# Sparse attention and a Mish MLP on one core: two products joined into one of 129 columns, in another order of work

## The chip, the cores and the metric

One core of a Trainium2 chip runs the whole program. The metric is the time of one execution on the device in microseconds; lower is better. The engines are PE (TensorE; its weight loads are PEld), DVE (VectorE), ACT (ScalarE), POOL (GpSimd) and SP (SyncE, which here only issues DMAs).

## What is computed

Block-sparse attention over 4 batches, 8 heads, 768 positions, 64 dimensions per head, and then an MLP without biases over the 3072 resulting rows of 512:

```python
block, n_blocks = 32, 24
scores = (q @ k.T) / 8
# a block of 32 queries sees: its neighbours (distance <= 1), the first and the last block,
# and 3 sampled blocks; the first and the last block of queries see everything
scores = where(mask, scores, -1e9)
attn = exp(scores - max); attn = attn / (sum(attn) + 1e-9)
x = (attn @ v) laid out as [3072, 512]
h = x @ w_in                       # [3072, 2048]
out = (h * tanh(softplus(h))) @ w_out
```

All inputs are float32. The kernel multiplies in float16 in three products: every operand is split into a high and a low half, and high by high, low by high and high by low are added up in float32.

## The kernel before

**Attention** is cut into 52 jobs, 13 for each batch. Two of the 13 are dense (the first and the last block of queries, 768 keys each, in three steps of 256, `nt = 3`; of these jobs 0, 10, 13, 23, 26, 36, 39 and 49); the other 44 are pairs of neighbouring query blocks (`nt = 2`, one step for each block, 256 gathered keys each). A job is a chain over the engines. PE computes the scores S of all 8 heads (L674); DVE takes the maximum (L737); ACT the exponential into pt (L756); PE transposes (L680); ACT writes the high half of the transposed probabilities, ph (L779), DVE the low half, pl (L783; up to job 5 PE subtracts in PSUM and ACT copies, L787 and L792). Then PE does the O block (L818): with 32 columns of ph or pl as weights on one of four column strips, it multiplies gathered values. A row of values holds, for each head, 64 high halves, a one, 64 low halves and a zero, so a product of 65 columns gives the output's high part and the sum of the probabilities in one, and another of 64 columns the part of the low halves. All O blocks write the same PSUM bank, `obank`; a job has up to four regions in it, numbered by the query block w and the half g of a pair of heads. DVE then takes the reciprocal of the sums and scales (`xs_fn`: r at L837, L838, xs at L840), PE transposes back (tx, L680 again), and ACT and DVE split the result into the halves xh and xl (L864, L867), which the MLP reads.

**The MLP** runs over 12 tiles of 256 rows, two passes on PE: h (L1068, eight steps of 2 x 12 products) and y (L1162). The last four tiles use a folded form of the second pass (L1281: seven products over sums of blocks instead of eight, some of them in obank). Between the passes ACT, DVE and POOL compute Mish (L1079 to L1148) and the halves g and, for the folded form, the sums' halves sg (L1144 and L1148).

**Weights** come in by DMA (`load_w`, L893; w_in as wr, w_out as wor), and are decoded and split by DVE and ACT before the first product of L1068 (L901 to L907, L962, L968; gsc at L1035).

**Order.** Every step is a task with a number. `Plan.add` registers it with its engine, and for some a second possible engine; `ORDER`, a table of numbers at the end of the file, says in which order the tasks are written out and, with a letter b, that the second engine does it. Each engine executes its instructions strictly in that order, waits included; DMA issues stand in the streams of SP or ACT. In a word such as `172+33` the number after the plus makes `fill` (L1502 on) issue that many products of 240 columns into columns of obank that nobody reads, ahead of the task; they stand only where no O block is open. A constant `SPLIT = 10` says from which job on an O block is one task instead of one for each step.

The O block and the scaling, as they were:

```python
o, w = tl[ko], 0 if dense else j                 # obank as [P, 2, 2, 66]
for n, (p, v0, v1) in enumerate(((hi, 0, D + 1), (hi, D + 1, 2 * D + 1), (lo, 0, D + 1))):
    for c in range(NPR):
        nc.tensor.matmul(o[cs, w, g, 0:v1 - v0], p[:, k, g, cs], vt[:, k, 2 * c + g, v0:v1], ...)
...
nc.vector.tensor_tensor(out=xs, in0=o[:, 0:nsu, :, 0:D], in1=r.unsqueeze(3).to_broadcast([P, nsu, 2, D]), op=ALU.mult)
```

Of the kernel before, what the change touches and what calls it, by code (L numbers as in the profile page):

```python
# [14 lines left out]
ALU = mybir.AluOpType  # L15
# [6 lines left out]
PSC = 4096.0  # L22
# [197 lines left out]
def attn_mish_kernel(ctx: ExitStack, tc: tile.TileContext, qT, kT, v, sampled, blocks, w_in, w_out, out):  # L220
# [119 lines left out]
    NO, NZ = 4 * (D + 2), 240  # L340
# [315 lines left out]

# [41 lines left out]
    def attend(job):  # L698
# [108 lines left out]
        def o_fn(j):  # L807
            if j == 0:
                tl[ko] = obank[:, 0:NO].rearrange("p (w g d) -> p w g d", w=2, g=2)
            o, w = tl[ko], 0 if dense else j  # L810
            vt = vgs[sus[w]["ng"] % NVG] if not dense else tl["vt", b, j] if sus[0]["qb"] else tl["v", b, j]
            hi, lo = tl["ph", i, j], tl["pl", i, j]
            for g in range(2):
                for k in range(2):
                    for n, (p, v0, v1) in enumerate(((hi, 0, D + 1), (hi, D + 1, 2 * D + 1), (lo, 0, D + 1))):
                        for c in range(NPR):
                            cs = slice(c * BS, (c + 1) * BS)
                            nc.tensor.matmul(  # L818
                                o[cs, w, g, 0:v1 - v0], p[:, k, g, cs], vt[:, k, 2 * c + g, v0:v1],
                                start=j == 0 and g == 0 and k == 0 and n == 0,  # L820
                                stop=j == nt - 1 and g == 1 and k == 1 and n == 2)
# [12 lines left out]
        def xs_fn():  # L834
            o = tl[ko]
            r = new(sb, "r", ("r", i), [P, nsu, 2])
            nc.vector.tensor_scalar(out=r, in0=o[:, 0:nsu, :, D], scalar1=PSC * 1e-9, scalar2=None, op0=ALU.add)  # L837
            nc.vector.reciprocal(out=r, in_=r)  # L838
            xs = new(at_, "xs", ("xs", i), [P, nsu, 2, D])
            nc.vector.tensor_tensor(  # L840
                out=xs, in0=o[:, 0:nsu, :, 0:D], in1=r.unsqueeze(3).to_broadcast([P, nsu, 2, D]), op=ALU.mult)
        add("DVE", 0.8, xs_fn, r=[ko], w=[("r", i), ("xs", i)], new=[("r", ("r", i)), ("xs", ("xs", i))], key=-1.5)

        def tx_fn():
            tx = new(ps["t"], "t", ("tx", i), [P, nsu, P])
            for w in range(nsu):
                transpose(tx[:, w], tl["xs", i][:, w].rearrange("p g d -> p (g d)"), w == 0, w == nsu - 1)
# [721 lines left out]
    456 484 1629 268b 506 439 1638 457 440 485 257 486 235 1640 243 248 487 1630 488 253 441 164 458 442 489 459 482  # L1569
    510 1631b 254 1639 1641 511 529 1632 460 527 81 512 289 491 490 1651 500 492 285 78 1633 269 493 507 461 1652 513  # L1570
    249 1634 1642 290 514 515 258 494 286 462 495 1653 509 255 531 1643 270 1654 259 1635b 250 463 516 528 1655 1636
    496 501 517 518 532 1665 519 591 1656 272b 520 533 276b 497 1657 1644 291 292 89 521 251 498 522 1645 530 534 499
    293 523 1666 535 271 536 1668 1658 537 280b 273 1646 548 1659 538 524 1669 525 1667 526 1647 287 294 539 593 1660
    1679 1648 540 1680 1661 541 1649b 1662 551 1670 542 1650 552 1663b 543 1684 550 1671 549 544 1664 1685 553 1681
    554 295 1697 274 555 281 277 1698 275 1686 1672 464 1687 556 278 559 1702 279 560 557 561 1673b 296 282 297 298
    1688 299 1699 562 283 1674 300 1703 1689 558 563 1675 564 301 302 303 545 1717 1676 546 465 547 565 1704 304 1677
    466 1678 305 588 1718 306 467 566 590 307 1722 309b 1690 308 1723 310 1719 1691 313b 468 1735 311 469 314 1724 502
    1736 317 503 318 504 1740 312 321 1692 315 1682 1705 322 316 1683 325 505 470 1741 319 326 570 320 329 1695 323
    330 1696 324 333 589 327 334 592 567 1700 328 337 331 338 595 1725 332 1701 596 614 335 594 568 336 597 1713 598
    611 569 615 634 1714 599 612 90 1706 571 600 473b 1715 603 617 1716 604 613 601 1720 1707 618 572 602 619 1721 573  # L1580
    476b 605 620 606 1726 471 1733 616 1727b 477b 574 472 1734 621 575 607 1708 622 625 623 1693 1738 626 624 1694
    1728 627 1739 474 608 1729 576 478 628 1737 1751 629 609 610 475 630 1752 631 1709 632 1755 580 1753b 1710 1742
    1758 584 1730 1711b 585 640 636 635 1756 581 641 1712 1731b 1760 1743 582 1759 642 1757 665 659 577 586 1761 1754
# [127 lines left out]
```

## Time and profile before

| | |
|---|---|
| median of 3 runs | 754.28 us (751.87 to 755.23) |
| profiled execution | 754.41 us, its span 752.6 us |
| busy: PE, PEld, DVE, ACT, POOL | 708.4, 543.4, 548.1, 579.3, 281.7 us |
| mean granted clock of PE | 0.984 |
| chain that ended last, by engine | PE 82%, DVE 7%, DMA 4%, issue 3% |
| O blocks, S blocks on that chain | 6%, 5% |

The span is one execution's first to last instruction; 1.8 us of the execution lie around it. Granted clock 1.00 is 2.4 GHz, 0.50 is 1.2 GHz. A busy PE counts a product from its start to its modelled end, and since products overlap, what one costs in a row of them is read from the distance of their starts, as the chain of waits gives it. "issue" is time in which an engine waited for nothing that the profile shows.

### The profile page before, as it was taken

To read this page: it belongs to the slowest core of one execution; us is meant where nothing else is said; L and a number is where in the kernel's file an instruction comes from. 1 tells how busy PE (TensorE), PEld (TensorE's weight loads), DVE (VectorE), ACT (ScalarE), POOL (GpSimd) and SP (SyncE) were. 2 spreads that over 40 slices of the span, in tenths; PEclk is the share of its full clock that TensorE was granted. 3 is DMA by queue.
4 is the path that set the end of the run, shared out by engine and by line. 5 is a ranking of instruction groups with operands and counts; after the bars stand their busy time and mean duration, and the time that the engine had idled before them with its cause. 6 is when DMAs were issued, how large, how long until landed. Compare 5 with 4: busy or idle time off the path is not lost.

```text
span 752.6 us, 31176 instructions
## 1 busy us (share of the span) xinstructions
PE 708.4 (94%) x13023; PEld 543.4 (72%) x13023; DVE 548.1 (73%) x1015; ACT 579.3 (77%) x927; POOL 281.7 (37%) x380
## 2 busy tenths in 40 slices
PE   5567798999999999999999999999999999999997
PEld 4455577875776776777676776677677778888887
DVE  5869878897667856977767757877886855577665
ACT  2648677999796788887877789886887786787783
POOL 2004234517754551244543454564374301200140
PEclk9889899999999999999999999999999999999999
DMA  8788766533235273247337353344532447000001
GB/s 302 249 250 245 227 212 179 198 121 88 108 112 167 83 251 103 93 132 217 91 104 229 102 213 108 82 142 144 159 88 72 145 131 245 16 1 15 16 29 43
DMA packets 60050, 103.75 MB, mean 138 GB/s; under 512 B 8579, under 2 KB 20868, under 8 KB 59908
## 3 DMA queue, kind: packets, MB, share of 16 engines
q1 hardware_dynamic: 54576, 88.90, 37.9%
q10 hardware_dynamic: 5332, 12.85, 5.2%
q8 instruction: 102, 1.67, 0.9%
q14 instruction: 40, 0.33, 0.1%
HBM read 84.58 MB, written 17.14 MB: 135 GB/s over the span
## 4 chain that ended last, share of the span: by engine, by line
PE 82%; DVE 7%; DMA 4%; issue 3%; SPq 2%; ACT 1%; POOLq 0%; ACTq 0%; POOL 0%; DVEq 0%
PE h_None L1068 31%; PE y L1162 21%; PE yr L1281 8%; PE obank L818 6%; PE t L680 6%; PE s L674 5%; DMA vg<-vd 2%; PE obank L1281 1%; PE tx L680 1%; DMA raw_k<-in_k_dram 1%; DVE hs_None L1107 1%; DMA raw_q<-in_q_dram 1%; SPq L580 1%; DVE v L504 1%; ACT pt L756 1%
## 5 line engine op out<-in xcount | busy, mean ns | idle before, releaser
L1068 PEld LDWEIGHTS <-wi 128*128 128x128 f16 x2304 | 223.8, 98 | 38.6 <-issue 5.4
L1068 PE MATMUL h_None<-xh,wi 128*128 128x256 f16 x1152 | 208.1, 274 | 3.2 <-issue 3.2
L611 POOL COPY kg<-kt 128x256 f16 x246 | 112.5, 491 | 163.2 <-PE s L674 146.3
L1162 PE MATMUL y<-wo,g 128*128 128x512 f16 x672 | 159.1, 379 | 0.0
L1068 PE MATMUL h_None<-xl,wi 128*128 128x256 f16 x576 | 157.6, 274 | 0.0
L1120 POOL TENSOR_TENSOR g<-hs_None,g 128x1024 f16<-128x1024 f32 x36 | 81.0, 2251 | 131.3 <-ACT g L1114 85.7
L1162 PEld LDWEIGHTS <-g 128*128 128x128 f16 x768 | 74.1, 98 | 70.8 <-issue 1.1
L756 ACT ACTIVATE pt<-s,nb,ns 128x256 f32<-128x256 f32 (+1 forms) x208 | 107.4, 584 | 1.3 <-DVE wi L907 0.9
L779 ACT ACTIVATE ph<-t 128x512 f16<-128x512 f32 x112 | 66.1, 600 | 47.1 <-PE t L680 39.2
L783 DVE SCALAR_TENSOR_TENSOR pl<-t,ph 128x512 f16<-128x512 f32 x99 | 67.0, 684 | 35.0 <-ACT ph L779 34.8
L680 PE MATMUL t<-ident,pt 128*128 128x128 f32 x448 | 68.9, 280 | 9.3 <-ACT pl L792 4.4
L1107 DVE SCALAR_TENSOR_TENSOR hs_None<-us_None,hs_None 128x1024 f32<-128x1024 f32 x48 | 62.7, 1307 | 18.9 <-ACT us_None L1106 17.6
L1079 ACT ACTIVATE hs_None<-h_None,gsc 128x512 f32<-128x512 f32 x96 | 66.0, 687 | 13.6 <-PE h_None L1068 13.6
L737 DVE TENSOR_REDUCE mx<-s 128x4 f32<-128x1024 f32 x44 | 53.7, 1220 | 27.8 <-PE s L674 27.8
L1068 PE MATMUL h_None<-xr,wi 128*128 128x256 f16 x576 | 67.8, 273 | 0.0
L680 PEld LDWEIGHTS t<-ident,pt 128*128 128x128 f32 x448 | 52.3, 143 | 21.3 <-ACT pl L792 5.7
L818 PEld LDWEIGHTS <-ph 128*32 128x32 f16 x3584 | 47.8, 94 | 14.7 <-issue 12.9
L1098 ACT ACTIVATE us_None<-hs_None,hsc 128x1024 f32<-128x1024 f32 x48 | 55.4, 1154 | 1.6 <-DVE sg L1148 1.1
L818 PE MATMUL obank<-vg,ph 128*32 128x65 f16 (+1 forms) x3200 | 49.1, 196 | 2.6 <-issue 2.3
L1105 ACT ACTIVATE us_None<-us_None 128x1024 f32<-128x1024 f32 x48 | 50.9, 1059 | 0.3
L1106 ACT ACTIVATE us_None<-us_None 128x1024 f32<-128x1024 f32 x48 | 50.7, 1060 | 0.4
L818 PEld LDWEIGHTS <-pl 128*32 128x32 f16 x1792 | 46.5, 96 | 5.7 <-issue 3.8
(258 smaller groups left out, 1202.9 us busy)
## 6 DMA issues: line engine op xcount, KB each, us to landing
vg<-vd SPq DMA_DIRECT2D x320, 65.0 KB, 2.6
vg<-vd SPq DMA_DIRECT2D x80, 195.0 KB, 3.2
wr<-in_moe_w_in_dram ACTq DMA_DIRECT2D x7, 1024.0 KB, 6.3
vd<-v SPq DMA_DIRECT2D x12, 520.0 KB, 4.2
vg<-vd SPq DMA_DIRECT2D x12, 520.0 KB, 5.3
raw_k<-in_k_dram SPq DMA_DIRECT2D x12, 512.0 KB, 5.8
raw_q<-in_q_dram SPq DMA_DIRECT2D x12, 512.0 KB, 4.4
raw_v<-in_v_dram SPq DMA_DIRECT2D x12, 512.0 KB, 4.9
```

The source lines that it names most:

```text
L611: nc.gpsimd.tensor_copy(out=dst, in_=tl["kt", b][:, :, ds(j, BS)])
L680: nc.tensor.matmul(out, src, ident, start=start, stop=stop, is_transpose=True)
L756: ex = lambda o, x, g, w: nc.scalar.activation(out=o, in_=x, func=AF.Exp, bias=nb[:, g, w:w + 1], scale=tl["ns", b, sus[w]["qb"] // TB][:, ...
L779: nc.scalar.activation(out=new(at_, "ph", ("ph", i, j), [P, 2, 2, P], F16), in_=tl["t", i, j], func=AF.Copy, scale=PSC)
L783: nc.vector.scalar_tensor_tensor(out=new(at_, "pl", ("pl", i, j), [P, 2, 2, P], F16), in0=tl["t", i, j], scalar=PSC, in1=tl["ph", i, j], o ...
L818: nc.tensor.matmul(o[cs, w, g, 0:v1 - v0], p[:, k, g, cs], vt[:, k, 2 * c + g, v0:v1], start=j == 0 and g == 0 and k == 0 and n == 0, stop ...
L1068: nc.tensor.matmul(h[:, f2, 0:n].rearrange("p (s q) -> p s q", q=BS), wi[:, fp, w, cc, fs], x[:, s0:s0 + sn, cc], start=f2 == 0 and k == 0 ...
L1079: nc.scalar.activation(out=tl[kq][:, 2 * (fp % 2):2 * (fp % 2) + 2, 0:n], in_=tl[kh][:, :, 0:n], func=AF.Copy, scale=gsc[:, fp:fp + 1])
L1107: add("DVE", 1.32 * c, lambda: nc.vector.scalar_tensor_tensor(out=hs(), in0=us(), scalar=-0.5, in1=hs(), op0=ALU.add, op1=ALU.mult), r=[ku ...
L1120: add("POOL", 2.3 * c, lambda: nc.gpsimd.tensor_tensor(out=g(1), in0=hs(), in1=g(0), op=ALU.subtract), r=[kq, ("gh",) + kp], w=[kp], use=[kg],
L1162: nc.tensor.matmul(tl[ky], tl["g", b, t, k][:, g, f, q], wo_at(fc)[:, w], start=fc == 0 and n == 0, stop=fc == NFC - 1 and n == 2)
L1281: nc.tensor.matmul(R(i), lhs, rhs, start=head and j == n == 0, stop=k == NFC // 4 - 1 and j == 1 and n == 2, skip_group_check=True)
```

## The change

From job 10 on the products of ph with the high and with the low halves of the values are one product of 129 columns, in three of the four regions: 65 columns as before and right beside them the 64 of the low halves. The regions are then 130 columns apart in place of 66; the fourth has no room in the bank's 512 columns for the second part, and keeps the three products. The low part is no longer added up on PE; DVE scales it by r, too, and adds it (`add_lo`, two more instructions a job). xs becomes a flat tile of 7 x 64, of which the last three parts hold the scaled low part.

```diff
-    NO, NZ = 4 * (D + 2), 240
+    NO, NZ, OP = 4 * (D + 2), 240, (D + 2, 2 * (D + 1))
...
+    def add_lo(xs, t, o, r):
+        nc.vector.tensor_tensor(out=t, in0=o, in1=r, op=ALU.mult)
+        nc.vector.tensor_tensor(out=xs, in0=xs, in1=t, op=ALU.add)
...
-                tl[ko] = obank[:, 0:NO].rearrange("p (w g d) -> p w g d", w=2, g=2)
-            o, w = tl[ko], 0 if dense else j
+                tl[ko] = obank
+            w, apart = 0 if dense else j, i >= SPLIT
...
-            for g in range(2):
-                for k in range(2):
-                    for n, (p, v0, v1) in enumerate(((hi, 0, D + 1), (hi, D + 1, 2 * D + 1), (lo, 0, D + 1))):
-                        for c in range(NPR):
...
+            for g, k in ((g, k) for g in range(2) for k in range(2)):
+                at, whole = (OP[apart] * (2 * w + g), apart and w + g < 2)
+                prods = ((hi, 0, 2 * D + 1), (lo, 0, D + 1)) if whole else ((hi, 0, D + 1), (hi, D + 1, 2 * D + 1), (lo, 0, D + 1))
+                for n, (p, v0, v1) in enumerate(prods):
+                    for cs, c in ((slice(c * BS, (c + 1) * BS), c) for c in range(NPR)):
+                        nc.tensor.matmul(
+                            obank[cs, at:at + v1 - v0], p[:, k, g, cs], vt[:, k, 2 * c + g, v0:v1],
...
-            xs = new(at_, "xs", ("xs", i), [P, nsu, 2, D])
-            nc.vector.tensor_tensor(
-                out=xs, in0=o[:, 0:nsu, :, 0:D], in1=r.unsqueeze(3).to_broadcast([P, nsu, 2, D]), op=ALU.mult)
+            nc.vector.tensor_tensor(out=xs[:, 0:m], **dict(zip(("in0", "in1"), part(0, m))), op=ALU.mult)
+            add_lo(xs[:, 0:min(m, 3)], xs[:, 4:4 + min(m, 3)], *part(D + 1, min(m, 3))) if i >= SPLIT else None
...
 ORDER = """
-    7 1 0 8 2 9 3 4 53 74 5 6 67 10 85 11 12 14 51 13 15 18 76 16 17 28 92 19 20 22 117b 29 21 61 24 23 75 30+5 93 77
+    7 1 0 2 3 5 8 4 9 10 60 11 12 6 13 64 14 18 88 15 117b 16 20 69 17 19 93b 28 22 56 29 76 21 24 84 30 77 23 63 99b
```

The table ORDER is another one throughout, from another seed, and has no word with a plus. Counted over the whole program it moves, besides the above: all 17 weight loads of ACT's stream to SP's; 7 squares of L1103 from POOL to ACT (L1104), 4 copies of g from ACT to DVE (L1116), and a few more single steps from one engine to its second.

The O block of job 11, a pair, in PE's stream before (each row stands four times, once for each column strip, and the three groups again for the other seven combinations of query block, g and k):

```order
L818 LDWEIGHTS ph_11_0_5499
L818 MATMUL obank_109<-vg0_115,ph_11_0_5499 32x65
...
L818 MATMUL obank_109<-vg0_115,ph_11_0_5499 32x64
L818 LDWEIGHTS pl_11_0_5514
L818 MATMUL obank_109<-vg0_115,pl_11_0_5514 32x65
```

The same place in the change (the second half are the last rows of the block, the fourth region):

```order
L818 LDWEIGHTS ph_11_0_5327
L818 MATMUL obank_109<-vg0_115,ph_11_0_5327 32x129
L818 LDWEIGHTS pl_11_0_5366
L818 MATMUL obank_109<-vg0_115,pl_11_0_5366 32x65
...
L818 LDWEIGHTS ph_11_1_5350
L818 MATMUL obank_109<-vg1_116,ph_11_1_5350 32x65
L818 MATMUL obank_109<-vg1_116,ph_11_1_5350 32x64
L818 MATMUL obank_109<-vg1_116,pl_11_1_5352 32x65
```

Of 96 pairs of a weight load and a product 72 are left. In the whole program PE has 3584 products of 65 columns and 1792 of 64 before, 2408, 616 and 1176 of 129 after.

PE's stream around the transposes of job 0's output (tx_0), before, with two of the places at which fills (neg into obank) stand:

```order
L373 MATMUL gram_wi_1_1074<-wi_71 128x128
L396 MATMUL tp_w_0_1093<-wq_0_923,ones_69 128x2
L1506 LDWEIGHTS neg_73
L1506 MATMUL obank_109<-neg_73 128x240
L680 MATMUL tx_0_1109<-ident_64,xs_0_1091 128x128
...
L870 MATMUL tx_0_1109<-xh_0_0_1135,neg_73 128x128
```

and in the change:

```order
L373 MATMUL gram_wi_2_1091<-wi_71 128x128
L680 MATMUL t_1_1_1115<-ident_64,pt_1_866 128x128 x4
L680 MATMUL tx_0_1123<-ident_64,xs_0_1076 128x128
L674 LDWEIGHTS q_0_0_305
L674 MATMUL s_2_1128<-kt_0_230,q_0_0_305 32x96
```

The fills are gone here and everywhere (113 of them), and S of job 2 follows at once.

ACT's stream while jobs 0 and 1 run, before, with two of the weight loads (wr):

```order
L608 ACTIVATE kg1_114<-kt_0_259 128x8x32
L893 DMA wr_4_1065<-in_moe_w_in_dram 128x4x512
L962 ACTIVATE wi_71<-wi_71,ws_0_1095 128x1024
...
L756 ACTIVATE pt_1_1138<-s_1_746,nb_1_1133,ns_0_0_277 128x256 x2
L893 DMA wr_7_1187<-in_moe_w_in_dram 128x4x512
L779 ACTIVATE ph_1_0_1288<-t_1_0_1179 128x512
```

and SP's in the change, where these loads stand now:

```order
L893 DMA wr_6_810<-in_moe_w_in_dram 128x4x512
L571 DMA vg1_116<-vd0_60 32x1040 x2
L571 DMA vg0_115<-vd0_60 32x1040 x2
L893 DMA wr_4_917<-in_moe_w_in_dram 128x4x512
L580 TENSOR_LOAD offv_87
...
L571 DMA vg2_117<-vd0_60 32x1040 x2
```

ACT's ph no longer stands behind a load; the gathers of values (vg) and the register loads (L580) do.

## Rows read from the trace of the kernel before

**Rows 1.** The page's part 1: busy time and share of each engine.

```profile
PE 708.4 (94%) x13023; PEld 543.4 (72%) x13023; DVE 548.1 (73%) x1015; ACT 579.3 (77%) x927; POOL 281.7 (37%) x380
```

**Rows 2.** Stretches: busy us and count of PE, PEld, DVE, ACT, POOL; granted clock; DMA.

```profile
60.00:85.00 25.00, 19.44 (x671) 14.34 (x656) 23.77 (x52) 20.28 (x44) 10.21 (x12) 1.00 0.85 265
90.60:92.10 1.50, 1.50 (x98) 1.30 (x98) 0.35 (x2) 1.46 (x4) 0.00 (x0) 0.50 0.56 163
300.00:350.00 50.00, 49.98 (x807) 36.94 (x807) 42.01 (x74) 40.53 (x64) 18.77 (x31) 1.00 0.48 151
500.00:622.00 122.00, 120.92 (x2555) 90.02 (x2553) 91.04 (x172) 96.95 (x162) 50.26 (x69) 1.00 0.41 120
```

**Rows 3.** The chain of waits, S and O blocks: start us, us, engine, tile, line.

```profile
110.11 0.93 PE s L674 x86
...
175.06 0.78 PE s L674 x48
...
178.53 0.94 PE obank L818 x92
...
192.44 1.10 PE s L674 x48
...
215.34 1.29 PE obank L818 x144
```

**Rows 4.** Instructions of line 1506, the fills: ns min/median/max, first and last start.

```profile
L1506 PE MATMUL obank<-neg x113: 262/266/408, 14.2 to 93.2; 128*128 128x240 f16 x113
```

**Rows 5.** The chain of waits before 94 us: first and last of its three pieces of fills.

```profile
64.20 0.47 PE obank L1506 x3
...
88.66 0.64 PE obank L1506 x3
```

**Rows 6.** The chain before 94 us: its first PE piece after 25 us, others at either clock.

```profile
51.97 0.53 PE t L787
...
68.60 0.45 PE t L680 x4
...
87.61 1.05 PE t L680 x4
...
90.62 1.46 PE s L674 x96
```

**Rows 7.** What PE waited for from 120 us on: us in total, times, longest.

```profile
PE h_None L1068 <- issue: 3.2, 4, 1.0
PE t L680 <- DVE pl L783: 0.5, 2, 0.3
PE obank L818 <- issue: 0.5, 2, 0.3
```

**Rows 8.** The page's part 3: the queue that brings PE's instructions (packets, MB).

```profile
q8 instruction: 102, 1.67, 0.9%
```

**Rows 9.** Instructions on DVE: the scaling xs, and an add from SBUF.

```profile
L840 DVE TENSOR_TENSOR xs<-obank,r x52: 291/424/425, 41.8 to 621.9; 128x256 f32<-128x256 f32 x44, 128x128 f32<-128x128 f32 x8
...
L1133 DVE TENSOR_TENSOR us_None<-hs_None x26: 414/418/426, 586.3 to 738.9; 128x256 f32<-128x256 f32 x26
```

**Rows 10.** What ACT waited for before 130 us: us in total, times, longest.

```profile
ACT ph L779 <- DMA vg<-vd: 4.6, 1, 4.6
...
ACT wi L962 <- DMA vg<-vd: 4.2, 1, 4.2
...
ACT ph L779 <- issue: 3.1, 1, 3.1
```

**Rows 11.** The timeline on ACT and DVE at the end: last copy of h, last sg.

```profile
728.51 0.69 ACT L1079 ACTIVATE hs_None<-h_None,gsc 128x512 f32<-128x512 f32 x1 [1.10 <-PE h_None L1068]
...
741.35 1.23 DVE L1148 TENSOR_TENSOR sg<-us_None,sg 128x1024 f16<-128x1024 f32 x1
```

**Rows 12.** The chain at the end: twelve products of h, six folded ones of y.

```profile
722.58 1.31 PE h_None L1068 x12
...
730.44 0.66 PE obank L1281 x6
```

More of the change, by code (lines that the diff above doesn't have):

```diff
@@ L808, in o_fn @@
             if j == 0:
-                tl[ko] = obank[:, 0:NO].rearrange("p (w g d) -> p w g d", w=2, g=2)
-            o, w = tl[ko], 0 if dense else j
+                tl[ko] = obank
+            w, apart = 0 if dense else j, i >= SPLIT
             vt = vgs[sus[w]["ng"] % NVG] if not dense else tl["vt", b, j] if sus[0]["qb"] else tl["v", b, j]
             hi, lo = tl["ph", i, j], tl["pl", i, j]
-            for g in range(2):
-                for k in range(2):
-                    for n, (p, v0, v1) in enumerate(((hi, 0, D + 1), (hi, D + 1, 2 * D + 1), (lo, 0, D + 1))):
-                        for c in range(NPR):
[L817 to L821, printed above, removed]
+            for g, k in ((g, k) for g in range(2) for k in range(2)):
[5 more added lines that the diff above has]
+                            obank[cs, at:at + v1 - v0], p[:, k, g, cs], vt[:, k, 2 * c + g, v0:v1],
+                            start=j == 0 and g == 0 and k == 0 and n == 0,
+                            stop=j == nt - 1 and g == 1 and k == 1 and n == len(prods) - 1)
         def rv(j):
@@ L834, in xs_fn @@
         def xs_fn():
-            o = tl[ko]
-            r = new(sb, "r", ("r", i), [P, nsu, 2])
-            nc.vector.tensor_scalar(out=r, in0=o[:, 0:nsu, :, D], scalar1=PSC * 1e-9, scalar2=None, op0=ALU.add)
+            o, d, m = obank[:, 0:D], OP[i >= SPLIT], 2 * nsu
+            r, xs = new(sb, "r", ("r", i), [P, m]), new(at_, "xs", ("xs", i), [P, 7, D])
+            nc.vector.tensor_scalar(out=r, in0=obank[:, D:D + d * (m - 1) + 1:d], scalar1=PSC * 1e-9, scalar2=None, op0=ALU.add)
             nc.vector.reciprocal(out=r, in_=r)
-            xs = new(at_, "xs", ("xs", i), [P, nsu, 2, D])
-            nc.vector.tensor_tensor(
-                out=xs, in0=o[:, 0:nsu, :, 0:D], in1=r.unsqueeze(3).to_broadcast([P, nsu, 2, D]), op=ALU.mult)
+            part = lambda at, n: (bass.AP(o.tensor, o.offset + at, [o.ap[0], [d, n], [1, D]]), r[:, 0:n].unsqueeze(2).to_broadcast([P, n, D]))
+            nc.vector.tensor_tensor(out=xs[:, 0:m], **dict(zip(("in0", "in1"), part(0, m))), op=ALU.mult)
+            add_lo(xs[:, 0:min(m, 3)], xs[:, 4:4 + min(m, 3)], *part(D + 1, min(m, 3))) if i >= SPLIT else None
         add("DVE", 0.8, xs_fn, r=[ko], w=[("r", i), ("xs", i)], new=[("r", ("r", i)), ("xs", ("xs", i))], key=-1.5)
@@ L1569 @@
[L1569 to L1583, printed above, removed]
@@ new lines @@
+    1371 2142 1361 1313 2153 2126 1314 1620 1395 1362 2152 1394 2127 2326b 1337 1378 2154 1391 2143 1363 2156 1392
+    1379 2128 1380 2155 2158 2144 1338 1397 1339 1381 1364 1398 1413 2157 1374 1340 1399 2129b 1414 1365 1383 2145b
+    2159 2130 1382 1384 1393 2173 2146 1346 1400 2174 1416 1385 1401 1366 1402 1367 2169 2147 1368 1417 2175 1419 1403
+    1386 1420 1441 2170 1396 1445 1421 1444 1387 1422 1405 2178 2327 2171b 1406 1435 2160 2179 2148 1415 2161 1442
+    2176 1407 1423 2162 1424 1404 2172 2191 1425 2180 1447 2181 1408 1448 1466 2163b 1427 1418 2177 1467 1449 1428
@@ new lines @@
+    2474 2430 2432 2480 2459 2445 2518 2433 2460 2478 2431b 2481 2476 2461b 2523 2434b 2525 2496 2482 2462 2483 2519
+    2545 2463 2502 2484b 2546 2464 2497 2485 2467 2500 2503 1621 2468 2498 2517 2469b 2486 2504 2541 2505 2524 2506
+    2543 2520 2507 2487 2508b 2526 2542 2509 2490 2544 2488 2548 2549 2521 2489b 2491 2550 2510 2527 2492 2551 2552
+    2522 2528 2465 2511 2547 2529 2559 2514 2560 2556 2553 2466b 2583 2577 2554 2561 2562 2557 2555 2530 2449 2558
+    2576 2298 2512 2531 2452 2563 2532b 2513 2578 2533 2564 2584 2534 2601 2579 2535 2585 2538 2580 2515 2600 2536
@@ L1668 @@
+    2646b 2679 2686 2685 2693 2690 2687 2691 2694 2689 2684 2696 2692 2697 2700 2681 2698 2701 2688 2699 2695 2702
 """
```

176 lines of the change are left out of this document (96 added, 80 removed), and 21 rows, old and new, of the table ORDER.

## The prediction

> **What bounds the kernel now.** I read the engine shares first, then a table by stretches, then the chain of waits, then what PE waits for. The engine shares give PE 708.4 us of 752.6 (94%), against 548.1 for DVE and 579.3 for ACT [rows 1]. The stretches show that this is two programs. Up to about 120 us PE has idle time (busy 19.44 of 25 us at 60 to 85, fills included) and DVE is nearly full (23.77 of 25); from there to the end PE is busy 49.98 of 50 us and 120.92 of 122 [rows 2]. In that second part the three largest sums of PE's waits come to 4.2 us, and another engine stands in them with half a microsecond [rows 7]. So after 120 us a microsecond taken off PE's own instructions is a microsecond of the run; before 120 us it is not, unless it lies on the chain.
>
> The profiled execution took 754.41 us, 0.1 us from the median of the three runs shown (754.28), with a span of 752.6; all sums are made against 754.4.
>
> **The change part by part.**
>
> *Fewer products on PE (L818).* From job 10 on there are 35 pair jobs and 7 dense jobs (10, 13, 23, 26, 36, 39, 49). A pair job's O block goes from 96 weight loads and products to 72, a dense job's from 144 to 96: 35 x 24 + 7 x 48 = 1176 fewer. The columns that PE streams are the same: 40 x 65 + 8 x 64 + 24 x 129 = 6208 where there were 64 x 65 + 32 x 64 = 6208. So the question is whether a block costs by products or by columns. The trace has the same choice made once already, in the S blocks: with 96 narrow products the block takes 0.93 us, with 48 wide ones over the same columns (48 x 256 against 48 x 96 + 48 x 160) it takes 0.78 [rows 3]. Fewer products do help, but not in proportion (that would be 0.47). An O block of 96 takes 0.94 us [rows 3], and its 6208 columns on four column strips (1552 each) are the load that S puts on eight (12288 / 8 = 1536). I therefore take 0.78 us as what the columns alone cost, and 0.94 x 72 / 96 = 0.71 as what the products alone would cost; the larger counts: 0.78. That saves 0.16 a block, 35 x 0.16 = 5.6 us. A dense O block takes 1.29 us now; a dense S block with nearly its columns (18432 / 8 = 2304 against 9312 / 4 = 2328) takes 1.10 [rows 3], so 7 x 0.19 = 1.3 us more. Together **-6.9 us**, all of it after 120 us. Ends: nothing, if 129 columns cost just what 65 and 64 cost; and -11.2, if cost goes by products (35 x 0.235 + 7 x 0.43).
>
> The Trainium skill (TensorE: Matmul & The Clock Gate, section "Wait — 56ns, not 53.3ns?") says that the distance between the starts of two matmuls never falls below about 25 ns however small they are; by that 1176 of them would be an estimated 29 us. The trace does not agree: 0.94 us for 96 is 9.8 ns each [rows 3], so the measurement decides and this enters nothing.
>
> *No fills.* The 113 products of 240 columns into the O bank all stand between 14.2 and 93.2 us [rows 4], where PE has room, so their 18 us of PE time are not in the sum. On the chain lie three pieces of them, 0.47 us at first and 0.64 at last [rows 5], 1.5 us together; these go. What they did is keep PE's clock up. In the stretch of 60 to 85 us, with fills throughout, the granted clock is 1.00 (2.4 GHz); at 90.6 to 92.1 it is 0.50 (1.2 GHz), after a stretch in which PE had been waiting [rows 2]. The same work costs 0.93 against 1.46 us for an S block [rows 3, 6] and 0.45 against 1.05 for four transposes [rows 6]. Without fills PE has 18 pieces, 10.7 us, on the chain between 25 and 94 us, from 51.97 to 90.62 [rows 6]; some 5.7 us of these ran at the high level, and at the low level, by 1.46 / 0.93, they would be 3.2 us more. **+1.7 us** (-1.5 + 3.2). Ends: -1.5 if the clock holds by itself, and +12.3 if each of the six jobs that lead to the first MLP product were delayed in turn (0.53 for S, 2 x 0.6 for the transposes, about 0.5 for O: 2.3 x 6 = 13.8, less 1.5).
>
> *Weight loads from ACT's queue to SP's.* All 17 loads of L893 that ACT issued go to SP, in between V gathers and register loads. In the trace ACT stood still behind them three times: 4.6, 4.2 and 3.1 us, each time with a finished input for its next instruction [rows 10]. That cover for DVE and PE is gone: ACT's exponentials and splits of jobs 1 to 6 can start earlier. What is late next is DVE, which is full there [rows 2], and the V gathers, which now stand behind loads that wait for a free buffer. I take **-1.5 us** of the 11.9; ends -5 (somewhat under half of the waits reach the chain) and +4 (one V gather comes a wait of 4 us later).
>
> *Two more DVE instructions a job (L657, L658).* The trace has no 192-wide row; the scale of 256 from PSUM takes 424 ns, of 128 takes 291, and a 256-wide add from SBUF 418 [rows 9], so about 0.36 each: 35 x 0.72 + 7 x 0.58 = 29 us. DVE has 8 us of 50 free in its fullest stretch, about 42.0 busy [rows 2], and four jobs add 2.9 there: covered. PE needs the result at the job's transposes (tx). In the new order 2.6 us or more of PE work stand between O and tx in every job from 10 on but the last (12 products of L1068, 1.3 us [rows 12]); the chain r, reciprocal, scale, two more is about 1.5 us. So 0, except **+0.3 us** at job 51. If the cover is gone PE waits 0.7 us a job; ends 0 and +4.
>
> *Less code.* PE's queue loses 1176 + 113 pairs, 2578 of its 26046 rows. PE waited 3.2 + 0.5 us after 120 us for nothing the profile shows ("issue") [rows 7], at places where many short instructions had just gone by; the instruction queue moved 102 packets, 1.67 MB, which is 64 bytes for each PE row [rows 8]. Ten per cent fewer rows: **-0.5 us**, ends -3.7 and +2 (the boundaries fall elsewhere).
>
> *The order.* All engines' streams are permuted. At the first MLP product the two orders have put the same jobs through S (0 to 6) and through O (0 to 4), and the same number of DVE decodes before gsc, so I see no shift of the start. At the end I do: after the last L1068 product PE had 22 folded products before the first one on the last g, 24 before the last sg; now 18 and 20. ACT's last copy of h starts at 728.51 and the last sg is done at 741.35 + 1.23 = 742.58, 14.1 us later [rows 11]; 20 folded products, six matmuls and 0.66 us each [rows 12], are 13.1. **+1.0 us**. Elsewhere 0, ends -3 and +5.
>
> Sum: 754.4 - 6.9 + 1.7 - 1.5 + 0.3 - 0.5 + 1.0 = **748.5 us**.
>
> **The rivals.**
>
> *Columns alone (same).* If PE streams 129 columns in the time of 65 and 64, the first term is 0: 755.4 us. For it: in S the halving of the products saved only 0.15 of 0.93. Against it: it did save that, and O is further from its columns (0.94 against 0.78) than S at 48.
>
> *A cold start (slower).* Without fills the clock stays at 1.2 GHz until the MLP begins, at about 94 us; the price is the upper end above, 12.3 for 1.7: 759.1 us. It decides if more than about 10 us of the 13.8 reach the first L1068 product. For it: the granted clock is down to 0.50 even with fills [rows 2]. Against it: DVE, not PE, is full at 60 to 85 [rows 2], and a job's delay runs beside the next job's. The Trainium skill (TensorE: Matmul & The Clock Gate, section "Part 1: The HAM clock gate (the "warmup" mystery)") says that the throttled state is the default and activity releases it, which speaks against taking fills out; the trace agrees as far as the low clock at 90.6 us goes.
>
> *The order starves PE (same).* DVE carries 29 us more, and single waits of PE for DVE appear after 120 us, 0.2 a job more on average: +8, 756.5 us.
>
> *The start gains (faster still).* ACT without its waits brings the first MLP product forward by 5 us in place of 1.5, the clock holds by itself (-1.5 for +1.7) and the code waits go (-3.7 for -0.5): 738.6 us.
>
> *Nothing happens.* That the products are not joined is ruled out by the order of the program: 1176 rows of 129 columns stand there.
>
> **How the numbers follow.** 0.5% is 3.8 us, about what a measurement of this kernel can tell from no change: faster is below 750.5, slower above 758.1. The forecast has 0.55, with its own range of 743 to 753; four fifths of it lie below 750.5. Columns alone 0.12, cold start 0.11, starved order 0.10 (a fifth of it above 758.1), the early gain 0.12. Faster: 0.44 + 0.12 = 0.56; same: 0.11 + 0.12 + 0.08 = 0.31; slower: 0.11 + 0.02 = 0.13. The range of 741 to 758 leaves out the cold start (0.11) and the far half of the early gain (0.06).
>
> **What would show it.** Right: O blocks of pair jobs near 0.78 us and dense ones near 1.10 in the chain, PE still over 98% busy after 120 us, the first L1068 product within 3 us of its 94 us, no ACT wait of over 2 us behind a load, granted clock below 1.00 in more of the first 90 us. Wrong: O blocks still at 0.9 or more (columns alone); the first L1068 product past 100 us (cold start); rows of PE waiting for DVE r or xs (starved).

## The result and the profile after

The change takes 746.17 us (median of 19 runs) where the kernel before, beside it, took 754.05 (19 runs): ratio 0.9891, 95% interval 0.9869 to 0.9914, or 8.2 us less by the ratio (7.9 by the medians). Every ratio here leaves out the times that lie over 1.5% above the fastest of the same kernel, in this pair one of the 19 on each side. The prediction was 5.9 us less.

| | before | after |
|---|---|---|
| span of the profiled execution | 752.6 | 744.4 |
| first product of L1068 starts at | 93.7 | 86.2 |
| from there to the end of the span | 658.9 | 658.2 |
| mean granted clock of PE | 0.984 | 0.970 |

So, in these two executions, 7.5 of the 8.2 us are there before the MLP begins, and behind it only 0.7 are left. The engine shares and the instruction queue of the change (the page's parts 1 and 3):

```profile
PE 694.8 (93%) x11734; PEld 531.7 (71%) x11734; DVE 589.6 (79%) x1105; ACT 583.1 (78%) x928; POOL 277.4 (37%) x373
...
q8 instruction: 92, 1.51, 0.8%
```

PE has 1289 products fewer than in [rows 1] (1176 + 113), DVE 41.5 us more, and the instruction queue ten packets fewer than in [rows 8]. Two stretches from a table by stretches of the change (columns as in [rows 2]; the first answers to its first row, the second to its third):

```profile
60.00:85.00 25.00, 16.54 (x581) 12.18 (x588) 18.74 (x51) 16.35 (x37) 3.85 (x10) 0.76 0.81 228
300.00:350.00 50.00, 48.91 (x785) 35.95 (x772) 45.62 (x86) 42.70 (x67) 17.30 (x29) 1.00 0.42 122
```

Without fills the clock is at 0.76 in the first, as foreseen, and still the first product of L1068 is early. DVE is no longer full there (18.74 of 25 us against 23.77): it has done more before. Its busy time up to 60 us, in two stretches of before

```profile
0.00:25.00 25.00, 15.94 (x162) 12.95 (x163) 13.44 (x47) 11.31 (x13) 5.29 (x19) 1.00 0.87 305
25.00:60.00 35.00, 20.25 (x562) 15.94 (x561) 28.14 (x50) 18.20 (x39) 1.52 (x3) 0.80 0.77 234
```

and of the change:

```profile
0.00:25.00 25.00, 9.47 (x110) 7.71 (x110) 17.33 (x51) 11.50 (x14) 5.79 (x19) 0.87 0.88 310
25.00:60.00 35.00, 24.89 (x691) 18.96 (x695) 33.36 (x58) 25.93 (x53) 6.97 (x7) 0.75 0.89 263
```

That is 41.6 us of DVE work before and 50.7 after. The chain of waits in the change, an O block of a dense job and one of a pair, answering to [rows 3]:

```profile
204.97 1.16 PE obank L818 x85
...
216.00 0.83 PE obank L818 x69
```

They take 1.16 us where 1.29 stood and 0.83 where 0.94 stood; in PE's timeline the pair blocks lie between 0.82 and 0.84, but for two (2.09 and 3.10) in or behind which PE waits. What PE waited for from 120 us on in the change (as [rows 7]):

```profile
PE tx L680 <- DVE xs L658: 2.1, 3, 1.3
PE t L680 <- DVE pl L783: 2.0, 2, 1.1
PE obank L818 <- DMA vg<-vd: 1.9, 2, 1.5
PE t L680 <- issue: 1.2, 1, 1.2
PE s L674 <- DVE kg L615: 0.5, 1, 0.5
PE t L680 <- DVE xl L867: 0.4, 1, 0.4
PE h_None L1068 <- issue: 0.4, 1, 0.4
```

The waits for nothing that the profile shows ("issue") fall from 4.0 us (3.7 in [rows 7] and 0.3 at L680) to 1.6, and in their place PE waits for DVE (5.0 us in four rows, 0.5 before) and for gathered values (1.9, 0.3 before).

### The profile page after: what moved, and what is told of

Its sections match the earlier page's. It is cut to its first block, busy times and chain, and to the rows that moved or that the text cites. A ratio compares the mean times of both kernels' runs of the same rounds, so it can differ in the third digit from the quotient of the medians.

```text
span 744.4 us, 28682 instructions
## 1 busy us (share of the span) xinstructions
PE 694.8 (93%) x11734; PEld 531.7 (71%) x11734; DVE 589.6 (79%) x1105; ACT 583.1 (78%) x928; POOL 277.4 (37%) x373
## 4 chain that ended last, share of the span: by engine, by line
PE 79%; DVE 10%; DMA 6%; SPq 2%; issue 2%; ACT 0%; DVEq 0%
PE h_None L1068 29%; PE y L1162 20%; PE yr L1281 8%; PE t L680 6%; PE obank L818 5%; PE s L674 5%; DMA vg<-vd 3%; SPq L580 2%; PE tx L680 2%; DMA wor<-in_moe_w_out_dram 1%; PE obank L1281 1%; DVE xs L658 1%; DMA wr<-in_moe_w_in_dram 1%; DVE mx L737 1%; DVE v L504 1%
## 5 line engine op out<-in xcount | busy, mean ns | idle before, releaser
L1068 PEld LDWEIGHTS <-wi 128*128 128x128 f16 x2304 | 224.1, 98 | 35.1 <-issue 2.6
L1068 PE MATMUL h_None<-xh,wi 128*128 128x256 f16 x1152 | 206.6, 273 | 0.7 <-issue 0.7
L611 POOL COPY kg<-kt 128x256 f16 x246 | 118.9, 513 | 214.5 <-PE s L674 201.3
L1068 PE MATMUL h_None<-xl,wi 128*128 128x256 f16 x576 | 157.4, 273 | 0.5 <-issue 0.5
L1120 POOL TENSOR_TENSOR g<-hs_None,g 128x1024 f16<-128x1024 f32 x35 | 76.8, 2197 | 79.9 <-DVE g L1116 47.4
L680 PE MATMUL t<-ident,pt 128*128 128x128 f32 x448 | 72.6, 290 | 11.5 <-ACT pt L756 6.2
L1107 DVE SCALAR_TENSOR_TENSOR hs_None<-us_None,hs_None 128x1024 f32<-128x1024 f32 x48 | 60.4, 1257 | 19.8 <-ACT us_None L1106 19.8
L680 PEld LDWEIGHTS t<-ident,pt 128*128 128x128 f32 x448 | 55.1, 149 | 23.0 <-issue 10.3
L1068 PE MATMUL h_None<-xr,wi 128*128 128x256 f16 x576 | 68.8, 273 | 0.0
L818 PEld LDWEIGHTS <-ph 128*32 128x32 f16 x2408 | 43.4, 98 | 20.5 <-issue 9.6
L1105 ACT ACTIVATE us_None<-us_None 128x1024 f32<-128x1024 f32 x48 | 50.7, 1057 | 4.1 <-POOL us_None L1103 3.7
L818 PE MATMUL obank<-vg,ph 128*32 128x129 f16 (+2 forms) x2168 | 46.6, 211 | 6.8 <-DMA vg<-vd 6.5
L1106 ACT ACTIVATE us_None<-us_None 128x1024 f32<-128x1024 f32 x48 | 50.7, 1057 | 0.4
L1104 ACT ACTIVATE us_None<-us_None 128x1024 f32<-128x1024 f32 x39 | 41.1, 1054 | 9.2 <-DVE us_None L1101 9.2
```

Of the source, the lines that this page charges most:

```text
L611: nc.gpsimd.tensor_copy(out=dst, in_=tl["kt", b][:, :, ds(j, BS)])
L680: nc.tensor.matmul(out, src, ident, start=start, stop=stop, is_transpose=True)
L818: nc.tensor.matmul(obank[cs, at:at + v1 - v0], p[:, k, g, cs], vt[:, k, 2 * c + g, v0:v1], start=j == 0 and g == 0 and k == 0 and n == 0, ...
L1068: nc.tensor.matmul(h[:, f2, 0:n].rearrange("p (s q) -> p s q", q=BS), wi[:, fp, w, cc, fs], x[:, s0:s0 + sn, cc], start=f2 == 0 and k == 0 ...
L1120: add("POOL", 2.3 * c, lambda: nc.gpsimd.tensor_tensor(out=g(1), in0=hs(), in1=g(0), op=ALU.subtract), r=[kq, ("gh",) + kp], w=[kp], use=[kg],
```

## Experiments

In what follows a stop is a wait of PE put down to "issue". Sums of stops are taken from PE's waits from 86 us on: 8.0 us before, 2.3 in the change. Before:

```profile
PE obank L818 <- issue: 4.5, 4, 2.1
PE h_None L1068 <- issue: 3.2, 4, 1.0
...
PE t L680 <- issue: 0.3, 1, 0.3
```

and in the change, with the gathers from there on:

```profile
PE obank L818 <- DMA vg<-vd: 3.9, 4, 1.8
...
PE t L680 <- issue: 1.2, 1, 1.2
PE h_None L1068 <- issue: 1.1, 3, 0.5
```

### 1. What is the join's, what the order's?

e1 is the kernel before with the change's table; e2 is the change with the old one. The first line of the table stands for all of it.

```diff
 ORDER = """
-    7 1 0 8 2 9 3 4 53 74 5 6 67 10 85 11 12 14 51 13 15 18 76 16 17 28 92 19 20 22 117b 29 21 61 24 23 75 30+5 93 77
+    7 1 0 2 3 5 8 4 9 10 60 11 12 6 13 64 14 18 88 15 117b 16 20 69 17 19 93b 28 22 56 29 76 21 24 84 30 77 23 63 99b
```

> The change with its join undone: the new order (no fills, loads on SP), but three products everywhere and no added DVE instructions. Theory S (the start): the 7.5 us by which the first product of L1068 comes earlier are the order's, and the 4.8 us that the joined products save in the O blocks are given back to waits for the added DVE work; then this kernel has its first L1068 product near 86 us, O blocks at 0.94 us, and 745 to 748 us (ratio 0.988 to 0.993). Theory J (the join): the joined products are worth most of the gain; then 751 to 753 us (0.995 to 0.999).

> The old order with its fills and loads, only the products joined (and the two DVE instructions a job added). Theory S: first L1068 product still near 94 us, O blocks at 0.83 us, of the 4.8 us saved at most 2 left: 752 to 755 us (ratio 0.997 to 1.002). Theory J: 747 to 749 us (0.990 to 0.994), since the gain is the join's and needs no order.

Measured: e1 1.0003 (0.9967 to 1.0040), e2 1.0044 (1.0014 to 1.0074). Both theories fall: neither part alone has a gain that shows, and the join alone costs 3 us. The start did go with the order (first product of L1068 at 85.7 us in e1, 92.3 in e2). But e1 loses it again; its waits of PE from 86 us on:

```profile
PE obank L818 <- issue: 8.8, 3, 3.7
PE h_None L1068 <- issue: 5.0, 4, 1.7
PE obank L818 <- DMA vg<-vd: 1.7, 4, 0.7
PE t L680 <- issue: 1.4, 1, 1.4
```

15.2 us of stops. In e2 the stops are 7.2 us, near those of before, but PE waits for DVE, in the rows from 0.6 us up for 8.1 us:

```profile
PE t L680 <- DVE pl L783: 3.2, 4, 1.7
...
PE tp_q L396 <- DVE pl L783: 1.7, 1, 1.7
PE tx L680 <- DVE xs L658: 0.9, 3, 0.3
PE tx L680 <- DVE pl L783: 0.9, 3, 0.5
PE tx L680 <- DVE xl L867: 0.8, 1, 0.8
...
PE tp_k L396 <- DVE xl L867: 0.6, 1, 0.6
```

The two DVE instructions a job are the rival "the order starves PE" here: in an order made without them, PE's transposes stand too early. The change's table has room for them, though not everywhere.

### 2. The fills away, and the start alone

e3 is the kernel before with every plus taken out of the table. e4 has the products apart, the change's words up to the first product of L1068 (word 1623), and then the remaining words in the old order, without fills.

```diff
-    99 25 49 54 27 31 32+6 167 26 69 33 34 38 202 64 39 168 192 42 35 56 52 118 169 170 36 119 37 171 60 94 43 62
+    99 25 49 54 27 31 32 167 26 69 33 34 38 202 64 39 168 192 42 35 56 52 118 169 170 36 119 37 171 60 94 43 62
```

> The kernel before without its 113 fills, all else as it was. If the fills' work on the clock is worth more than their 1.5 us on the chain (cold start, the prediction's step): first L1068 product 1 to 5 us later than 94, 755 to 759 us (ratio 1.001 to 1.006). If they only stood in the way: first L1068 product up to 2 us earlier, 751 to 754 us (0.996 to 1.000). If they explain the start's gain: near 88 us, 747 to 749 us.

> The products apart as before; the new order up to the first product of L1068, and the old order for everything behind it. Theory S: first L1068 product near 86 us and 745 to 748 us (ratio 0.988 to 0.993), as the start is worth 7 to 8 us whatever follows. Theory J: near 86 us too, but the later work takes the 7 us back in waits: 752 to 755 us (0.997 to 1.002).

Measured: e3 1.0117 (1.0081 to 1.0152), 9 us slower and more than any theory had; e4 1.0081 (1.0049 to 1.0112), though its first product of L1068 stands at 85.6 us. In e3 the loss isn't at the start (first product of L1068 at 91.9 us, 1.8 earlier than before). It is in stops:

```profile
PE h_None L1068 <- issue: 8.5, 9, 1.6
PE obank L818 <- issue: 5.7, 7, 2.2
...
PE s L674 <- issue: 0.8, 2, 0.5
PE y L1162 <- issue: 0.7, 2, 0.5
```

Those are 15.7 us, among MLP products that no clock of the first 94 us can reach. Behind the start e3 and e4 have the same order, and their two longest later stops stand at the same places. PE's timeline at two of them (start, us, then engine, line and what; in brackets the idle time before), e3 first:

```profile
382.07 0.25 PE L818 MATMUL obank<-vg,ph 128*32 128x65 f16 x8 [2.02 <-issue]
...
610.67 0.21 PE L818 MATMUL obank<-vg,pl 128*32 128x65 f16 x1 [2.19 <-issue]
```

and e4:

```profile
384.80 0.21 PE L818 MATMUL obank<-vg,pl 128*32 128x65 f16 x2 [2.32 <-issue]
...
613.15 0.21 PE L818 MATMUL obank<-vg,pl 128*32 128x65 f16 x2 [1.80 <-issue]
```

These stops lie inside O blocks, in both kernels within one row of the same place of PE's stream. A row is here one instruction of PE's stream in the trace: a weight load, a product, or one of the 129 to 134 semaphore and drain instructions. Counted so, for some of the larger stops:

| kernel | stop ends at, us | rows of PE's stream before it | remainder by 256 |
|---|---|---|---|
| before | 119.67, 257.19, 381.81 | 4289, 9665, 14528 | 193, 193, 192 |
| change | 250.26 | 8897 | 193 |
| e1 | 116.65, 251.88, 392.93 | 4289, 9409, 14785 | 193, 193, 193 |
| e2 | 118.98, 349.35 | 4289, 11968 | 193, 192 |
| e3 | 112.24, 382.07, 610.67 | 3776, 14273, 22976 | 192, 193, 192 |
| e4 | 111.75, 384.80, 613.15 | 3777, 14272, 22977 | 193, 192, 193 |

The remainder is 192 or 193 at every stop from 86 us on, in these six traces and in those of all the runs below: 115 stops, 119.7 us in all, and not one elsewhere. The instruction queue's numbers fit: 1.67 MB in 102 packets is 16.4 KB each, and the 26176 rows of the kernel before are 102.25 times 256; the 23599 of the change are 92.2 times 256, and its queue moved 92 packets [rows 8]. So PE stops where its stream passes from one packet of 256 rows to the next. How long depends on how fast it got there. Worked out from PE's rows in eight traces (before, the change, e1 to e4, and e6 and e7 below), behind 130 us, PE came to 77 crossings less than 3 us after it had gone on from the one before, and these hold 42.2 us of stops; the 558 others hold 7.7.

The Trainium skill (Runtime: NRT & Kernel Launch, section "Instruction fetch mechanics") says that instructions come in blocks of 16 KiB, 256 of them, and that crossing a boundary is mostly hidden, since an engine dispatches slower than the blocks arrive. The traces agree on the block. On the hiding they differ where rows are short: 192 rows of an O block in 0.94 us [rows 3] are 4.9 ns each, and there a crossing cost up to 3.73 us (e1).

### 3. Rows without work

That the places of these rows decide is theory R; rival C is that the fills' work held the clock. e5 keeps the rows of the fills and takes their work; e6 and e7 add rows near 20 us, where PE waits for job 0's exponential, to the change and to e3:

```diff
-        for _ in range(n):
+        for m in range(n):
...
-            nc.tensor.matmul(obank[:, NO:NO + NZ], neg[:, 0], neg.rearrange("p n q -> p (n q)")[:, 0:NZ],
-                             start=True, stop=True)
+            cs = slice(m % 4 * BS, (m % 4 + 1) * BS)
+            nc.tensor.matmul(obank[cs, NO:NO + 2], neg[:, 0, cs], neg[:, 0, 0:2], start=True, stop=True)
...
-    171 100 41 172 85 94 44 173 174 95 176 45 73 204 177 67 96 175 49 184 339b 101 147b 180 205 193 178 181 194 182
+    171 100 41 172+54 85 94 44 173 174 95 176 45 73 204 177 67 96 175 49 184 339b 101 147b 180 205 193 178 181 194 182
```

The word 172+54 is e6's; e7 has 172+97.

> The kernel before with its 113 fills left at their places, but cut to 2 columns on one column strip: the rows of PE's stream are those of before, the fills' work is gone. Theory R (rows): in the six traces so far nearly all of PE's waits for nothing that the profile shows stand where its stream passes a multiple of 256 rows (16 KB, one packet of the instruction queue), and they are long where the 256 rows before took under some 3.3 us. Then this kernel keeps the places of before and takes 751 to 757 us beside 754 of the kernel before (ratio 0.996 to 1.003). Theory C (clock): the fills' work holds the clock, and it is as slow as the kernel without fills (ratio 1.009 to 1.015).

> The change, with 54 products of 2 columns (108 rows) put into PE's idle time near 20 us and nothing else changed. Theory R: the multiples of 256 rows fall elsewhere; worked out from the trace of the change with 3.3 us for 256 rows, the stops grow from 2.5 to 10.9 us, so 6 to 9 us more than the change: ratio to before 0.997 to 1.002, and issue waits of 8 to 12 us. If row positions do not matter: ratio 0.987 to 0.991, as the change itself.

> The kernel before without its fills, with 97 products of 2 columns (194 rows) near 20 us. Theory R: worked out as above the stops fall from 23.0 to 8.6 us against the kernel without fills alone (measured there: 18.4 in all); so 8 to 13 us less than it: ratio to before 0.994 to 1.003. Theory C: as slow as without fills alone, ratio 1.009 to 1.015.

Measured: e5 1.0002 (0.9978 to 1.0026): the fills' 18 us of work are worth nothing, their rows are worth the 9 us that e3 lost. Its own stops are at the same remainder, but longer than before (11.5 us for 8.0 in the two traces), so their size varies at the same rows. The clock did fall with the work, from 0.90 to 0.75 in the stretch of 60 to 94 us; e5:

```profile
60.00:94.00 34.00, 26.74 (x767) 19.41 (x766) 29.28 (x67) 24.98 (x53) 12.19 (x16) 0.75 0.77 225
```

e7 0.9934 (0.9901 to 0.9967): 97 empty pairs of rows make e3 14 us faster, and faster than the kernel before, with nothing joined. Its stops are 4.5 us, the largest of them:

```profile
PE obank L818 <- issue: 1.8, 3, 1.3
PE s L674 <- issue: 1.7, 1, 1.7
```

e6 0.9947 (0.9917 to 0.9977): the change with 54 empty pairs loses half of its gain, 4.2 us by the ratios (0.9947 against 0.9891; by the two intervals some 1.5 to 7). Its stops are 10.8 us, as worked out, but in an execution of 757.2 us, 5 over the median of e6. That they were 2.3 in the one trace of the change was lucky, since the same rows up to 180 us show more in e12 and e8 (5.2 and 6.0 in all), the difference all before 130 us. C has fallen. R holds: e5 came as expected, e7 a little beyond it, and e6 at about half of it, below the range that was given.

### 4. The weight loads

e8 takes the letter b from the 17 loads in the change's table, e9 gives it to them in the old one; PE's rows stay as they are.

```diff
-    7 1 0 8 2 9 3 4 53 74 5 6 67 10 85 11 12 14 51 13 15 18 76 16 17 28 92 19 20 22 117b 29 21 61 24 23 75 30+5 93 77
+    7 1 0 8 2 9 3 4 53 74 5 6 67 10 85 11 12 14 51 13 15 18 76 16 17 28 92 19 20 22 117b 29 21 61 24 23 75 30+5 93b 77
```

> The change with its 17 weight loads back in ACT's stream, at the places that the new order gives them; PE's rows are unchanged. Theory L (loads): they made the start: the first product of L1068 comes at 89 to 94 us in place of 86, ACT waits of over 2 us stand behind loads, ratio to before 0.993 to 1.000. Rival: the new sequence of DVE's and PE's early tasks made the start, and this kernel stays at 86 to 88 us and a ratio of 0.987 to 0.992.

> The kernel before, with nothing changed but that its 17 weight loads of ACT's stream stand in SP's, at the same places of the order; PE's rows and fills are unchanged. Theory L (ACT behind loads was what held the start): no ACT wait of over 2 us behind a load, the first product of L1068 at 87 to 91 us in place of 92 to 94, ratio to before 0.990 to 0.997. Rival: the loads on SP help only in the sequence of the new order, since in the old one they hold the gathers of values: first L1068 product at 92 to 97 us, ratio 0.998 to 1.004.

Measured: e8 1.0010 (0.9979 to 1.0041), e9 0.9945 (0.9922 to 0.9968). The first product of L1068, in e8 and e9:

```profile
L1068 PE MATMUL h_None<-xh,wi x1152: 269/273/421, 90.7 to 601.9; 128*128 128x256 f16 x192
```

```profile
L1068 PE MATMUL h_None<-xh,wi x1152: 269/273/283, 90.6 to 595.7; 128*128 128x256 f16 x192
```

So the loads on SP bring it forward by 4.5 us in the change (90.7 to 86.2) and by 3.1 in the old order (93.7 to 90.6). ACT's waits behind loads are back in e8 (2.8 and 2.5 us where [rows 10] had 4.6, 4.2 and 3.1) and gone in e9 and in the change. In time they are worth 4 us there and, by the ratios, 9 here; of the 9, 4.5 are the start, and the rest lies in stops (6.0 for 2.3) and in PE's waits for ACT's pl (2.1 us). The stops need not be the loads' doing: e12, with its loads on SP, has 5.2.

### 5. Put together

e10 is e4 with 97 pairs of rows at 20 us, so that its crossings fall as in e7. e11 and e12 are the change with the PE task behind a wait of PE moved ahead of it: five times in e12, one of them below (1752, a piece of y, ahead of 630, the transposes of job 12), and in e11 also S of job 9.

```diff
-    629 1708 584 1751 475 1709 630 1752 631 1742 632 576 580 636 1727b 640 1710 581 1755 668 1753 577 1711 1756 641
+    629 1708 584 1751 475 1709 1752 630 631 1742 632 576 580 636 1727b 640 1710 581 1755 668 1753 577 1711 1756 641
```

> Products apart, the new order up to the first product of L1068, the old order behind it, and 97 pairs of rows near 20 us so that the multiples of 256 rows fall as in the kernel without fills and with 97 pairs. Theory R and L together: the start at 85 to 87 us as in the same kernel without the rows, and its stops for rows fall from 14 to 3 or 4 us: 742 to 748 us (ratio 0.984 to 0.992), as fast as the change without joining anything. If the start's gain is always taken back later: ratio 0.993 to 1.000, as the kernel without fills and with 97 pairs.

> The change, with six tasks of PE moved ahead of one on which PE waited for DVE or a gather after 100 us (1.34, 1.09, 0.54, 0.96, 1.9 and 1.8 us in its trace): a piece of y or S, or transposes, now stand ahead of the transposes of job 12, 24, 37, 42 and of the O blocks of jobs 31 and 7. If those waits were real time: 4 to 7 us less, 739 to 742 us (ratio to before 0.979 to 0.985). If they only move elsewhere: ratio 0.986 to 0.991, as the change.

> As the kernel with six moved tasks, without the sixth (S of job 9 stays behind the O block of job 7), so that everything up to 180 us is the change's own order. The six moves gave single times from 737.5 to 751.8 us, too far apart to say what they are worth. If the five later waits (1.34, 1.09, 0.54, 0.96 and 1.9 us in the change's trace) are real time: 3 to 6 us less than the change, ratio to before 0.981 to 0.986, and none of the five is over 0.5 us in its trace, beyond what a later gather leaves. If not: 0.986 to 0.991.

Measured: e10 0.9921 (0.9899 to 0.9943): 12 us less than e4 by rows that do nothing, with the start at 86.8 us and stops of 4.5. It comes within reach of the change without a joined product. e11 has single times from 737.5 to 751.8 and a median of 747.31 beside 756.51 (0.988); its ratio of 0.9814 (0.9774 to 0.9853) rests on three of the six, so what its moves are worth stays open. In its trace a stop of 3.4 us stands at 87.9 us, and the first product of L1068 comes at 89.2. e12 measured 0.9845 (0.9802 to 0.9888), median 744.48, span 741.4, the fastest of the profiled kernels. What PE still waits for from 120 us on in e12:

```profile
PE obank L818 <- DMA vg<-vd: 1.4, 1, 1.4
PE t L680 <- issue: 1.2, 1, 1.2
PE s L674 <- DVE kg L615: 0.5, 1, 0.5
PE t L680 <- DVE xl L867: 0.4, 1, 0.4
PE tx L680 <- DVE pl L783: 0.2, 1, 0.2
PE tx L680 <- DVE xs L658: 0.2, 1, 0.2
```

Four of the five waits are gone; that for the gather at job 31 still takes 1.4 of its 1.9 us. That e11 and e12 beat the kernel before is shown: their slowest times are 751.82 and 747.46 us, its fastest beside them 753.48 and 750.72; that e12 beats the change is likely (3.5 us between the ratios) and not shown, for the intervals overlap.

## Why the prediction was right, and where not

The time and the sign hold, and the time lies in the range of the likeliest case; but the sum came out by errors that cancel. Of the signs of being right, the O blocks and the ACT waits came, and the first product of L1068 within 3 us of 94 did not (86.2); of the signs of being wrong, waits of PE for xs came (2.1 us). By its steps:

- **Fewer products: -6.9 forecast, -4.9 measured.** The mechanism is right, the size was off: 0.83 and 1.16 us a block, not 0.78 and 1.10, so 35 x 0.11 + 7 x 0.15 (the dense blocks took 1.29 to 1.34 before, 1.31 in the median). O blocks on four strips did not come down to the price of S blocks on eight.
- **No fills: +1.7 forecast, 0 measured** (e5, interval -1.7 to +2). That was measured in the old order. The lower clock that the cold start rival names is there, but the first product of L1068 comes at 92.2 us in e5, no later than before; DVE is busy for 29.28 of the 34 us from 60 to 94, so that it rather than PE sets the pace is likely.
- **Loads off ACT's queue: -1.5 forecast, -4 in the old order (e9) and -9 in the new (e8).** This is the term that was most too small, together with the next. That "somewhat under half of the waits" reach the chain was the end of the range and turned out the likelier value. The rival of an early gain has its place here: "I see no shift of the start" was wrong: the start gained 7.5 us, of which the loads explain 3 to 4.5. Another 2.1 are a stop that ends at 87.25 us in the trace of before, on the chain just ahead of the first product of L1068, and that the change does not have. The rest goes with the new sequence and was not taken apart.
- **Two DVE instructions: +0.3 forecast, 4.5 us more waits for DVE behind 120 us.** The price was right in the median only (0.35 and 0.36 us): the mean of the add L658 is 0.65, and the two cost DVE 41.4 us, not 29. What failed with it is the cover. Two waits of 1.3 and 0.5 us stand at tx, each behind an add that took 2.30 and 1.44 us (the last section has both); at 0.36 it would have been done before PE came there. Of the two waits for pl (1.1 and 1.0) the first stands in e1 too (0.9), without the added work. Some of it comes back elsewhere, since e12 removes most of these waits and gains perhaps 3.5 us.
- **Less code: -0.5 forecast, with ends -3.7 and +2; -5.7 in the two traces.** The step that failed. It took ten per cent fewer rows for ten per cent fewer stops. What counts is where the crossings fall: 226 rows less at the start cost 9 us (e3), 194 empty ones gave 14 (e7). The stops fell from 8.0 to 2.3 us, of which 3.6 behind the first product of L1068; some 3 us of the fall may be the luck of that one trace of the change (section 3).
- **The order: +1.0 forecast for the end, 0 measured, and nothing forecast elsewhere.** From the last PE product to the end of the span are 3.8 us in both; PE met no wait for the last g and sg. Elsewhere PE waits 3.6 us more for gathered values. That the loads on SP hold these gathers is not shown: e8, with the loads on ACT, has 2.7 us of such waits.

What is behind the 0.7 us from the first product of L1068 on, then: -4.9 for products, -3.6 for stops, +4.5 for DVE, +3.6 for gathers, -1.4 for a wait for ACT's exponential that is gone; the remaining 1.1 us are not assigned.

The join seems to be worth what it is by rows as much as by longer products. In the change's order it makes 8.4 us (e1 against the change), where the blocks themselves save 4.9: with 72 pairs for 96 fewer crossings fall into a rush of short rows (behind 130 us 3 crossings in under 3 us in the change, 8 in e1). No run has e1's order with empty rows added, so this split is argued, not shown. That the positions in the change are favourable is seen from others: e1 has 15.2 us of stops and e6 10.8. The kernel before lies in the middle, with 8.0 where e3 has 15.7 and e7 4.5.

## What to carry to other kernels

Where an engine runs many short instructions, count its rows: each crossing of 256 that comes within about 3 us of the last may stop it, here for up to 3.7 us and for 0.55 on average, so an edit that adds or removes rows early moves the cost of everything behind it. Test an edit with its rows kept (empty instructions in the place of those removed), or with two or three paddings, before its effect is put down to its work. And a DMA issue that may wait for a buffer is better put on a queue that computes nothing: here that gave 4 us (e9).

## What the runs showed of the hardware that was not expected

Stops at 256 rows are the first thing. The second is the price of L658, the add of two SBUF operands: its median is 359 ns, but its longest 2298; L657, of the same width with an operand from PSUM, never took over 349. In the change:

```profile
L657 DVE TENSOR_TENSOR xs<-obank,r x42: 280/347/349, 147.2 to 613.5; 128x192 f32<-128x192 f32 x35, 128x128 f32<-128x128 f32 x7
...
L658 DVE TENSOR_TENSOR xs<-xs x42: 292/359/2298, 147.5 to 613.9; 128x192 f32<-128x192 f32 x35, 128x128 f32<-128x128 f32 x7
```

The longest one is the one that PE waited for at job 12. DVE's and then POOL's timeline there:

```profile
178.53 0.42 DVE L840 TENSOR_TENSOR xs<-obank,r 128x256 f32<-128x256 f32 x1
178.87 0.35 DVE L657 TENSOR_TENSOR xs<-obank,r 128x192 f32<-128x192 f32 x1
179.25 2.30 DVE L658 TENSOR_TENSOR xs<-xs 128x192 f32<-128x192 f32 x1
```

```profile
177.02 2.14 POOL L535 TENSOR_TENSOR kt<-raw_k,kt 128x1024 f16<-128x1024 f32 x1
...
179.21 2.12 POOL L535 TENSOR_TENSOR kt<-raw_k,kt 128x1024 f16<-128x1024 f32 x1
```

The add ends 0.22 us after POOL's TENSOR_TENSOR does, and the scale and the product from PSUM just before it, with POOL at another of these, take their usual 0.42 and 0.35. In the same way 1.44 us at 477.53 stand beside a POOL instruction from 476.62 to 478.76. Over the whole trace of the change it is the same: the 24 adds that ran while POOL was idle took at most 360 ns; of the 18 beside a POOL instruction 14 took 454 to 2298 ns, and all ten over 1 us stand beside a TENSOR_TENSOR of POOL. L657 ran beside one of those 14 times and took at most 348. So such an add on two SBUF operands can be held until one of POOL's instructions ends; no experiment varied it.
